# Batch 0 of a fused linear-attention and Swish kernel: by tiles, or by pairs of heads

## The chip, the cores and the metric

The kernel runs on one core of a Trainium2 chip. The metric is device microseconds of one execution. Before the change five runs gave a median of 295.37 us (295.13 to 296.06). Engines are called as in the profile: PE (TensorE), PEld (its weight loads), DVE (VectorE), ACT (ScalarE), POOL (GpSimd), SP (SyncE, which here only issues DMAs).

## The reference

Linear attention with phi(x) = elu(x) + 1, and behind it a feed-forward layer with a Swish whose slope differs per hidden unit:

```python
# q, k, v: (8 batches, 8 heads, 576, 64); w_in: (512, 2048); w_out: (2048, 512); beta: (2048,)
q_p, k_p = phi(q), phi(k)                       # phi(x) = where(x > 0, x, exp(x) - 1) + 1
kv  = einsum('bhsd,bhse->bhde', k_p, v)
z   = sum(k_p, axis=2)
num = einsum('bhsd,bhde->bhse', q_p, kv)
den = einsum('bhsd,bhd->bhs', q_p, z) + 1e-06
x   = (num / den) with the heads side by side   # (8 * 576, 512)
h   = x @ w_in
out = (h / (1 + exp(-beta * h))) @ w_out        # (4608, 512)
```

## The kernel before, in words

Everything is float32 in memory and bfloat16 on PE. A batch has 576 positions: four tiles of 128 and a tail tile of 64 (tile 4). The four tiles of a batch form xT[b], 512 channels by 512 positions; the tails of all eight batches are collected in xT_tail and computed as a ninth batch.

For each batch the order is: phi of k and q (an exp on ACT, a relu and a min on DVE: `phi_part`, `phi_relu`, `phi_min`, lines 134 to 154), kv and z on PE, numerators per tile on PE, the division by the denominator on DVE (`xs`), the transposes of x, then H: sixteen groups `ff` of 128 hidden units, each four matmuls over 512 positions (`h_mm`, line 321) and a Silu on ACT (`silu`), and then Y: four tiles, each four times four matmuls (`y_mm`, line 338), a copy out of PSUM and two output DMAs (`y_out`). Beta is folded in by scaling the Silu's input with beta and w_out's rows with 1/beta (`w_out_scale`).

The schedule is written out by hand: each engine runs its instructions in the order of the code, and waits on semaphores alone. From batch 2 on the attention steps of the next batch are put between the groups of H and Y by tables `sh` and `sy` (lines 629 to 652). Batches 0 and 1 are laid out by hand (lines 438 to 593), and the change is mostly there.

Loads. k of batch 0 goes by SP in float32 into `stage`, in two halves of four heads (line 93). q, v and all weights go by POOL's DMA queue, which casts to bfloat16: identities first (lines 98 to 101), then q and v of batch 0 in halves (lines 110 to 113), w_in in four quarters (line 118), later w_out, k, q and v of batches 1 and 2 (lines 447 to 452 and 531 to 533).

Heads. The 128 partitions hold two heads of 64 positions; index `hh` is the head's half on the partitions and `pr` a pair of heads on the free side, so `pr` = 0 gives channels 0 to 255 of x and `pr` = 1 channels 256 to 511 (`kc` = 0, 1 and 2, 3 of w_in).

Batch 0 in order on PE (lines 475 to 518): transposes of q for tiles 0 and 1 (`q_trans0`, copies on ACT), kv of pair 0 (`kv_direct` into kvp0), q's tile 2, den of tiles 0 and 1 (`dens`, then `recips` on DVE), kv of pair 1 (into kvp1), q's tile 3, numerators of tiles 0 and 1 (`numer0`: all 512 channels of a tile, one DVE multiplication into xs), q's tile 4, den of tiles 2 to 4, x's transposes of tiles 0 and 1 (`x_trans`, copies on ACT) around the numerators of tiles 2 and 3, then `h0_tile`: the first four groups of H tile by tile, 16 matmuls of 128 positions for each, with the transposes of tiles 2 and 3 (copies on DVE) and the numerator of tile 4 between. Then the four Silus, and groups 4 to 15 with all 512 positions; before group 6 stand the transposes of tile 4. PSUM has four buffers of tag "mm" in turn (warm_ps, two kvp0, dps, then the four h_ps, and so on), two "misc" ones for transposes and two "num0" ones for numerators: a later user of a buffer waits for the earlier one's reader.

Batch 0's Y and batch 1's attention are interwoven by hand (lines 537 to 593): Y's groups i = 0, 1 of all four tiles, group 2 of tile 0, z of batch 1, transposes of q for tiles 0 to 3, group 2 of tiles 1 and 2, q's tile 4, kv, den, `recips` and `kv_evac` on DVE, group 2 of tile 3 and group 3 of tile 0, the first numerators of batch 1.

ACT holds one table of functions at a time: in the profile an ACT_TABLE_LOAD stands where it changes between Exp and Silu. Copies run under either.

Of the kernel before, what the change touches and what calls it, by code (L numbers as in the profile page):

```python
# [16 lines left out]
def kernel(  # L17
# [61 lines left out]
    def load(eng, dst, src, b, h0=0, n=4):  # L79

        rows = src[b].rearrange("h (g j) d -> (h g) (j d)", j=J)
        return eng.dma_start(  # L82
            out=dst[:, h0 : h0 + n].rearrange("p h j d -> p h (j d)"),
            in_=rows.rearrange("(i p) e -> p i e", p=P)[:, h0 : h0 + n],
        )
# [9 lines left out]
    nc.vector.memset(warm, 0.5)  # L95
    tiny = consts.tile([P, 2], BF16)
    nc.scalar.activation(tiny[:, 0:1], warm[:, 0:1], ACTF.Exp)
    identity = consts.tile([P, P], BF16)
    make_identity(nc, identity)
    ident16 = consts.tile([FC, FC], F32)  # L100
# [7 lines left out]
    for i in range(2):  # L108
        nc.vector.memset(vaug[i][:, :, :, :, D : D + 2], 1.0)
    for h0 in (0, 2):  # L110
        load(nc.gpsimd, xq[0], q, 0, h0, 2)
    for h0 in (0, 2):
        load(nc.gpsimd, vb[0], v, 0, h0, 2)

    w_in_v = moe_w_in.rearrange("(c p) f -> p c f", p=P)
    w_out_v = moe_w_out.rearrange("(c p) m -> p c m", p=P)
    for i in range(4):
        nc.gpsimd.dma_start(out=w_in_sb[i], in_=w_in_v[:, :, i * 512 : (i + 1) * 512])

    def load_w_out(i):  # L120
        nc.gpsimd.dma_start(out=w_out_f[i], in_=w_out_v[:, i * 4 : (i + 1) * 4, :])
# [291 lines left out]
    def num0_tile():  # L413
        return num0ps.tile([P, 512], F32, tag="num0", name="nps0")
# [43 lines left out]
    idle(4)  # L458
    z_products(0, 1, zt)
    nc.vector.tensor_copy(beta_s, bps)  # L460
    nc.vector.tensor_mul(beta_m, beta_s, beta_s)
    nc.vector.tensor_scalar(beta_m, beta_m, TINY * TINY, 2.0 * TINY, ALU.is_lt, ALU.mult)
    nc.vector.tensor_add(beta_c, beta_s, beta_m)
    phi_step("q", 0, phi_relu)
    z_evac(zt)
    phi_step("q", 0, phi_min)
# [5 lines left out]
    def q_trans0(t):  # L472
        q_trans(0, (t,), misc_bf()[:, 0 : 512 if t < NT - 1 else 256], (nc.scalar,))

    q_trans0(0)
    q_trans0(1)
    kv_direct(0, 0, kvp0)
    for hh in range(2):
        kv_evac(0, hh, (0,), kvp0)
    q_trans0(2)  # L480
    dens(0, (0, 1), dps)
    recips(0, 2, P, dps)
    kvp1 = [num0_tile() for _ in range(2)]
    kv_direct(0, 1, kvp1)
    for hh in range(2):
        kv_evac(0, hh, (1,), kvp1)
    q_trans0(3)
    numer0(0, 0)
    numer0(0, 1)
    q_trans0(4)  # L490
    dens(0, (2, 3, 4), dps)
    x_trans(0, 0, nc.scalar)
    recips(2, 4, P, dps)
    recips(4, 5, G, dps)
    numer0(0, 2)
    x_trans(0, 1, nc.scalar)
    numer0(0, 3)
    hps = [mm_tile("h_ps") for _ in range(4)]

    def h0_tile(t):  # L500
        for ff in range(4):
            h_mm(0, xT[0], ff, hps[ff], t * P, (t + 1) * P)

    h0_tile(0)
    x_trans(0, 2, nc.vector)
    x_trans(0, 3, nc.vector)
    h0_tile(1)
    numer0(0, 4)
    h0_tile(2)
    h0_tile(3)  # L510
    for ff in range(4):
        silu(0, ff, hps[ff])
    for ff in range(4, FC):
        if ff == 6:
            x_trans(0, 4, nc.vector)
        hp = mm_tile("h_ps")
        h_mm(0, xT[0], ff, hp)
        silu(0, ff, hp)

    def w_out_scale(i, n_act):  # L520
        for c in range(4):
# [21 lines left out]
    kv1 = [miscps.tile([P, 512], F32, tag="misc", name="kv1") for _ in range(2)]  # L543
    kv_tile(1)
    y_mm(0, 0, 2, yps[0])
    for pr in range(2):
        z_products(1, pr, kv1)
    z_evac(kv1)
    w_out_scale(3, 0)
    for ts in ((0, 1), (2, 3)):  # L550
        q_trans(1, ts, num0_tile().bitcast(BF16), (nc.scalar, nc.scalar))
    y_mm(0, 1, 2, yps[1])
    y_mm(0, 2, 2, yps[2])
    dps1 = num0_tile()
    q_trans(1, (4,), dps1.bitcast(BF16)[:, 512:768], (nc.scalar,))
    for pr in range(2):
# [3 lines left out]
    recips(4, 5, G, dps1)  # L560
    for hh in range(2):
        kv_evac(1, hh, (0, 1), kv1)
    y_mm(0, 3, 2, yps[3])
    y_mm(0, 0, 3, yps[0])
    y_out(0, 0, yps[0], copier=nc.scalar)
    numer0(1, 0)
# [116 lines left out]
```

## Time and profile before

| what | value |
|---|---|
| median of 5 runs | 295.37 us (295.13 to 296.06) |
| the profiled execution | 296.06 us, its span 294.3 us |
| busy share of the span | PE 97%, PEld 49%, ACT 54%, DVE 40%, POOL 12% |
| matmuls of y (L341) | x600, 127.1 us busy, 370 ns of one |
| matmuls of h (L323) | x560 with xT, 118.3 us busy; x64 with the tails, 14.0 us |
| Silu (L331) | x144, 98.3 us busy, 688 ns of one |
| xs (L288, DVE) | x40, 27.2 us busy, 687 ns of one |
| first matmul of H in batch 0 | 17.11 us |
| first matmul of Y in batch 0 | 32.54 us |
| last piece of the chain that ended last | 290.14 us, copy of y on DVE |

All times in the timeline are microseconds from the span's start. A timeline row gives start, length from first start to last end, engine, line, operation, output and inputs, shape, how many instructions the row merges (x16), and in brackets how long the engine had been idle before it and who released it. A matmul's own length (0.38 for 512 columns, 0.22 for 128) is longer than its distance to the next (0.216 and 0.056), since matmuls are pipelined. A row of POOL or SPq with DMA_DIRECT2D is the issue of a DMA; it lands much later: q's two halves of batch 0 took a median of 7.7 us from issue to landing, w_in's quarters 13.8 us, w_out's up to 21 us. The digits in the page's second part are tenths of each of 40 slices of 7.4 us.

### The profile page before, as it was taken

To read this page: it belongs to the slowest core of one execution; us is meant where nothing else is said; L and a number is where in the kernel's file an instruction comes from. 1 tells how busy PE (TensorE), PEld (TensorE's weight loads), DVE (VectorE), ACT (ScalarE), POOL (GpSimd) and SP (SyncE) were. 2 spreads that over 40 slices of the span, in tenths; PEclk is the share of its full clock that TensorE was granted. 3 is DMA by queue.
4 is the path that set the end of the run, shared out by engine and by line. 5 is a ranking of instruction groups with operands and counts; after the bars stand their busy time and mean duration, and the time that the engine had idled before them with its cause. 6 is when DMAs were issued, how large, how long until landed. Compare 5 with 4: busy or idle time off the path is not lost.

```text
span 294.3 us, 4755 instructions
## 1 busy us (share of the span) xinstructions
PE 286.1 (97%) x1889; PEld 143.7 (49%) x1889; DVE 116.7 (40%) x268; ACT 158.6 (54%) x206; POOL 36.7 (12%) x54
## 2 busy tenths in 40 slices
PE   8899999999999999999999999999999999999994
PEld 3584457454445444544455445544554444444443
DVE  5663575835634461356135613652251200110021
ACT  5558685963936772578167916690671077017500
POOL 9532100320050005000500053000000000000000
PEclk9999999999999999999999999999999999999998
DMA  7999999489389949942993299717131310130033
GB/s 202 200 213 393 251 251 191 101 247 195 76 159 278 165 78 270 217 66 66 246 245 70 53 197 262 106 45 154 38 71 45 74 36 0 39 87 19 0 71 75
DMA packets 50887, 40.83 MB, mean 139 GB/s; under 512 B 30752, under 2 KB 42288, under 8 KB 50864
## 3 DMA queue, kind: packets, MB, share of 16 engines
q1 hardware_dynamic: 37968, 23.48, 33.8%
q0 software_dynamic: 12736, 16.91, 29.6%
q8 instruction: 15, 0.25, 0.3%
q10 hardware_dynamic: 160, 0.13, 0.2%
q14 instruction: 8, 0.07, 0.1%
HBM read 36.71 MB, written 9.44 MB: 157 GB/s over the span
## 4 chain that ended last, share of the span: by engine, by line
PE 84%; DMA 11%; ACT 2%; DVE 1%; POOL 1%; issue 1%; POOLq 0%; ACTq 0%
PE y_ps L341 39%; PE h_ps L323 38%; DMA xk<-in_k_dram 7%; DMA vf<-in_v_dram 3%; PE nps L274 2%; PE kvp L173 2%; ACT e L138 1%; POOL xq L82 1%; PE nps L421 0%; ACT L138 0%; PE xtp L304 0%; PE kv L184 0%; PE nps L242 0%; DVE y_sb L231 0%; DVE xs L288 0%
## 5 line engine op out<-in xcount | busy, mean ns | idle before, releaser
L331 ACT ACTIVATE g<-h_ps,beta_c 128x512 bf16<-128x512 f32 x144 | 98.3, 688 | 100.0 <-PE h_ps L323 100.0
L341 PE MATMUL y_ps<-w_out,g 128*128 128x512 bf16 (+3 forms) x600 | 127.1, 370 | 0.0
L323 PE MATMUL h_ps<-xT,w_in 128*128 128x512 bf16 (+1 forms) x560 | 118.3, 361 | 0.5 <-DVE y_sb L231 0.2
L341 PEld LDWEIGHTS <-g 128*128 128x128 bf16 x600 | 58.1, 98 | 64.7
L323 PEld LDWEIGHTS <-w_in 128*128 128x128 bf16 x624 | 56.7, 98 | 59.1 <-issue 0.7
L231 DVE COPY y_sb<-y_ps 128x512 f32<-128x512 f32 (+2 forms) x36 | 24.0, 672 | 82.5 <-PE y_ps L341 82.5
L288 DVE TENSOR_TENSOR xs<-nps,rden 128x512 bf16<-128x512 f32 (+1 forms) x40 | 27.2, 687 | 3.4 <-PE nps L421 1.8
L138 ACT ACTIVATE e<-xq 128x1152 bf16<-128x1152 bf16 (+2 forms) x17 | 18.0, 1100 | 2.3 <-DMA xq<-in_q_dram 2.3
L82 POOL DMA_DIRECT2D xk<-in_k_dram x7 | 5.2, 745 | 108.0 <-DMA qTd<-phi_q 81.3
L149 DVE TENSOR_TENSOR phi_q<-e,r 128x1152 bf16<-128x1152 bf16 (+2 forms) x17 | 12.1, 722 | 15.9 <-ACT e L138 15.6
L223 DVE TENSOR_TENSOR kv_bd<-kvp,kvmask 128x260 bf16<-128x260 f32 x12 | 4.6, 423 | 27.4 <-PE kvp L173 27.4
L138 ACT ACTIVATE e<-xk 128x1152 bf16<-128x1152 bf16 x14 | 15.4, 1149 | 0.0
L323 PE MATMUL h_ps<-xT_tail,w_in 128*128 128x512 bf16 x64 | 14.0, 379 | 0.0
L282 DVE TENSOR_SCALAR den<-nps 128x8 f32<-128x8 f32 (+1 forms) x30 | 4.9, 164 | 22.3 <-PE nps L274 22.3
L274 PEld LDWEIGHTS <-qTd 128*128 128x128 bf16 x120 | 9.3, 98 | 7.7 <-DVE xs L288 0.9
L149 DVE TENSOR_TENSOR phi_k<-e,r 128x1152 bf16<-128x1152 bf16 x16 | 11.5, 751 | 2.5 <-ACT e L138 2.3
L274 PE MATMUL nps<-kv_bd,qTd 128*128 128x130 bf16 x120 | 11.9, 221 | 0.4 <-DVE xs L288 0.4
L163 POOL CAST vaug<-vf 128x1152 bf16<-128x1152 f32 x10 | 11.2, 1159 | 2.2 <-DMA vf<-in_v_dram 2.2
L138 ACT ACT_TABLE_LOAD x6 | 7.7, 1283 | 5.6 <-DMA xq<-in_q_dram 3.8
L127 PE MATMUL warm_ps<-warm 128*128 128x512 bf16 x28 | 8.6, 465 | 1.5 <-DVE warm L95 1.5
L331 ACT ACT_TABLE_LOAD x7 | 9.0, 1283 | 0.1
L173 PEld LDWEIGHTS <-phi_k 64*128 64x128 bf16 x216 | 6.3, 94 | 2.5 <-issue 2.5
(69 smaller groups left out, 107.2 us busy)
## 6 DMA issues: line engine op xcount, KB each, us to landing
out_dram<-y_sb SPq DMA_DIRECT2D x70, 128.0 KB, 2.4
vf<-in_v_dram SPq DMA_DIRECT2D x5, 1152.0 KB, 6.2
xk<-in_k_dram POOLq DMA_DIRECT2D x7, 576.0 KB, 10.2
xq<-in_q_dram POOLq DMA_DIRECT2D x7, 576.0 KB, 13.0
w_in<-in_moe_w_in_dram POOLq DMA_DIRECT2D x4, 512.0 KB, 13.8
g<-in_moe_w_out_dram POOLq DMA_DIRECT2D x2, 1024.0 KB, 17.7
stage<-in_moe_w_out_dram POOLq DMA_DIRECT2D x2, 1024.0 KB, 21.0
stage<-in_k_dram SPq DMA_DIRECT2D x2, 576.0 KB, 4.1
```

Of the source, the lines that this page charges most:

```text
L82: return eng.dma_start(out=dst[:, h0 : h0 + n].rearrange("p h j d -> p h (j d)"), in_=rows.rearrange("(i p) e -> p i e", p=P)[:, h0 : h0 + n],
L127: nc.tensor.matmul(warm_ps[:, 0:cols], warm[:, 0:P], warm[:, 0:cols], start=True, stop=True)
L138: nc.scalar.activation(st[b, a, pr, "e"][:, :, j0:j1], x[:, :, j0:j1], ACTF.Exp)
L149: nc.vector.tensor_tensor(st[b, a][:, pr, j0:j1].rearrange("p j (h d) -> p j h d", h=2), st[b, a, pr, "e"][:, :, j0:j1].rearrange("p h j d ...
L163: eng.tensor_copy(vaug[b % 2][:, pr, :, :, 0:D], src[:, 2 * pr : 2 * pr + 2].rearrange("p h j d -> p j h d"),)
L173: nc.tensor.matmul(ps[hh, pr], st[b, "k"][r, pr, j, :], vaug[b % 2][r, pr, j, :, 0:EA], start=(j == 0), stop=(j == J - 1), skip_group_chec ...
L231: eng.tensor_copy(dst, src)
L274: nc.tensor.matmul(nps[: qs.shape[-1], hh, pr * 2 * EA : (pr + 1) * 2 * EA], qs, st[b, "kv"][:, hh, pr, :], start=True, stop=True, skip_gr ...
L288: nc.vector.tensor_mul(xs[:n].rearrange("p i a d -> p a i d"), num, rd[:, :, :, None].to_broadcast([n, 2, 4, D]),)
L323: nc.tensor.matmul(hp[:, c0:c1], w_in_sb[ff // 4][:, kc, (ff % 4) * P : (ff % 4 + 1) * P], x[:, kc, c0:c1], start=(kc == 0), stop=(kc == K ...
L331: nc.scalar.activation(g_sb[b % 2][:, ff, :], hp, ACTF.Silu, scale=beta_c[:, ff : ff + 1])
L341: nc.tensor.matmul(yp[:, c0:c1], g_sb[b % 2][:, ff, t * P : (t + 1) * P], w_out_sb[i][:, c, c0:c1], start=(ff == 0), stop=(ff == FC - 1), ...
```

## The change

Five edits:

- q's two loads of batch 0 are issued on POOL ahead of the identities and not behind them. w_in's first quarter is loaded in two calls, channels 0 to 255 and 256 to 511.
- Batch 0's tiles 0 to 3 go by halves of 256 channels. `numer_part` makes the numerators of two tiles for one pair of heads (and two half-width multiplications on DVE), `x_part` transposes one half of a tile (two transposes, one copy of 128x256, always on ACT), `h0_part` adds one half of a tile to the first four groups of H (eight matmuls). kv of pair 1 goes into the other columns of kvp0. den of tiles 0 and 1 now comes before q's tiles 2 and 3. A one-column Silu behind the second half copy loads ACT's table there. The three small DVE instructions for beta go behind the last multiplication.
- Tile 4 of batch 0 (q's transposes, den, numerator, x's transposes) moves into the groups of H behind `ff` = 5, 7, 8 and 10.
- In batch 0's Y, group 2 of tile 1 moves ahead of batch 1's z, group 2 of tile 2 ahead of the transposes of q, group 2 of tile 3 ahead of q's tile 4 (from behind `kv_evac`).
- In batch 1's H, kv of batch 2 goes behind group 8 and not 9, and the numerators start behind group 10 and not 11; the fourth and fifth and the DMA transposes of x follow in the groups of Y.

```diff
@@ loads @@
     nc.scalar.activation(tiny[:, 0:1], warm[:, 0:1], ACTF.Exp)
+    for h0 in (0, 2):
+        load(nc.gpsimd, xq[0], q, 0, h0, 2)
     identity = consts.tile([P, P], BF16)
     make_identity(nc, identity)
...
-    for h0 in (0, 2):
-        load(nc.gpsimd, xq[0], q, 0, h0, 2)
...
     for i in range(4):
-        nc.gpsimd.dma_start(out=w_in_sb[i], in_=w_in_v[:, :, i * 512 : (i + 1) * 512])
+        for c0, c1 in ((0, 2), (2, KC)) if i == 0 else ((0, KC),):
+            nc.gpsimd.dma_start(
+                out=w_in_sb[i][:, c0:c1], in_=w_in_v[:, c0:c1, i * 512 : (i + 1) * 512]
+            )
@@ batch 0 @@
     nc.vector.tensor_copy(beta_s, bps)
-    nc.vector.tensor_mul(beta_m, beta_s, beta_s)
-    nc.vector.tensor_scalar(beta_m, beta_m, TINY * TINY, 2.0 * TINY, ALU.is_lt, ALU.mult)
-    nc.vector.tensor_add(beta_c, beta_s, beta_m)
...
+    def numer_part(ts, pr):
+        nps = num0_tile()
+        for i, t in enumerate(ts):
+            for hh in range(2):
+                nc.tensor.matmul(
+                    nps[:, (i * 2 + hh) * P : (i * 2 + hh + 1) * P].rearrange(
+                        "p (h d) -> p h d", h=2
+                    ),
+                    q_stat(0, t, hh, pr, P),
+                    st[0, "kv"][:, hh, pr, :].rearrange("p (h e) -> p h e", h=2)[:, :, 0:D],
+                    start=True, stop=True, skip_group_check=True,
+                )
+        for i, t in enumerate(ts):
+            if pr == 0:
+                st[0, "xs", t] = work.tile([P, 4, 2, D], BF16, tag="xs", name="xs", bufs=4)
+            nc.vector.tensor_mul(
+                st[0, "xs", t][:, 2 * pr : 2 * pr + 2].rearrange("p i a d -> p a i d"),
+                nps[:, i * 256 : (i + 1) * 256].rearrange("p (a h d) -> p a h d", a=2, h=2),
+                rden0[:, t, :, 2 * pr : 2 * pr + 2, None].to_broadcast([P, 2, 2, D]),
+            )
+
+    def x_part(t, pr):
+        xv = st[0, "xs", t].rearrange("p i a d -> p (i a d)")
+        tp = misc_bf()[:, 0:256].rearrange("p (c t) -> p c t", c=2)
+        for c in range(2):
+            nc.tensor.matmul(
+                tp[:, c], xv[:, (2 * pr + c) * P : (2 * pr + c + 1) * P], identity,
+                is_transpose=True, start=True, stop=True, skip_group_check=True,
+            )
+        nc.scalar.copy(xT[0][:, 2 * pr : 2 * pr + 2, t * P : (t + 1) * P], tp)
+
+    def h0_part(t, pr):
+        for ff in range(4):
+            for kc in range(2 * pr, 2 * pr + 2):
+                nc.tensor.matmul(
+                    hps[ff][:, t * P : (t + 1) * P],
+                    w_in_sb[0][:, kc, ff * P : (ff + 1) * P],
+                    xT[0][:, kc, t * P : (t + 1) * P],
+                    start=(t == 0 and kc == 0), stop=(t == 3 and kc == KC - 1),
+                    skip_group_check=True,
+                )
...
     for hh in range(2):
         kv_evac(0, hh, (0,), kvp0)
-    q_trans0(2)
     dens(0, (0, 1), dps)
     recips(0, 2, P, dps)
-    kvp1 = [num0_tile() for _ in range(2)]
-    kv_direct(0, 1, kvp1)
+    q_trans0(2)
+    q_trans0(3)
+    numer_part((0, 1), 0)
+    kv_direct(0, 1, kvp0)
+    dens(0, (2, 3), dps)
     for hh in range(2):
-        kv_evac(0, hh, (1,), kvp1)
-    q_trans0(3)
-    numer0(0, 0)
...
+        kv_evac(0, hh, (1,), kvp0)
     recips(2, 4, P, dps)
...
+    x_part(0, 0)
+    x_part(1, 0)
+    nc.scalar.activation(tiny[:, 1:2], warm[:, 0:1], ACTF.Silu)
+    numer_part((0, 1), 1)
+    numer_part((2, 3), 0)
     hps = [mm_tile("h_ps") for _ in range(4)]
...
+    h0_part(0, 0)
+    x_part(0, 1)
+    h0_part(1, 0)
+    x_part(1, 1)
+    numer_part((2, 3), 1)
+    nc.vector.tensor_mul(beta_m, beta_s, beta_s)
+    nc.vector.tensor_scalar(beta_m, beta_m, TINY * TINY, 2.0 * TINY, ALU.is_lt, ALU.mult)
+    nc.vector.tensor_add(beta_c, beta_s, beta_m)
+    h0_part(0, 1)
+    x_part(2, 0)
+    h0_part(1, 1)
+    x_part(3, 0)
+    h0_part(2, 0)
+    x_part(2, 1)
+    h0_part(3, 0)
+    x_part(3, 1)
+    h0_part(2, 1)
+    h0_part(3, 1)
     for ff in range(4):
         silu(0, ff, hps[ff])
     for ff in range(4, FC):
-        if ff == 6:
-            x_trans(0, 4, nc.vector)
         hp = mm_tile("h_ps")
         h_mm(0, xT[0], ff, hp)
         silu(0, ff, hp)
+        if ff == 5:
+            q_trans0(4)
+        if ff == 7:
+            dps4 = num0_tile()
+            dens(0, (4,), dps4)
+            recips(4, 5, G, dps4)
+        if ff == 8:
+            numer0(0, 4)
+        if ff == 10:
+            x_trans(0, 4, nc.vector)
@@ batch 0's Y @@
     y_mm(0, 0, 2, yps[0])
+    y_mm(0, 1, 2, yps[1])
     for pr in range(2):
         z_products(1, pr, kv1)
     z_evac(kv1)
     w_out_scale(3, 0)
+    y_mm(0, 2, 2, yps[2])
     for ts in ((0, 1), (2, 3)):
         q_trans(1, ts, num0_tile().bitcast(BF16), (nc.scalar, nc.scalar))
-    y_mm(0, 1, 2, yps[1])
-    y_mm(0, 2, 2, yps[2])
+    y_mm(0, 3, 2, yps[3])
     dps1 = num0_tile()
...
         kv_evac(1, hh, (0, 1), kv1)
-    y_mm(0, 3, 2, yps[3])
     y_mm(0, 0, 3, yps[0])
@@ from batch 1 on @@
         if n < B:
-            at(sh, 9 if b == 1 else 4, lambda: kv_both(n))
+            at(sh, 8 if b == 1 else 4, lambda: kv_both(n))
             for t in range(NT):
-                ff = (11 if b == 1 else 5) + 2 * t
-                side, i = (sh, ff) if ff < FC else (sy, ff - FC - 1)
-                at(side, i, lambda t=t: numer(n, t))
-                side, i = (sh, ff + 1) if ff + 1 < FC else (sy, ff - FC + 1)
-                at(side, i, lambda t=t: x_trans_dma(n, t))
+                ff = (10 if b == 1 else 5) + 2 * t
+                for g, f in ((ff, numer), (ff + 1, x_trans_dma)):
+                    at(*((sh, g) if g < FC else (sy, g - FC)), lambda t=t, f=f: f(n, t))
```

More of the change, by code (lines that the diff above doesn't have):

```diff
@@ L479 @@
         kv_evac(0, hh, (0,), kvp0)
-    q_trans0(2)
     dens(0, (0, 1), dps)
     recips(0, 2, P, dps)
-    kvp1 = [num0_tile() for _ in range(2)]
-    kv_direct(0, 1, kvp1)
-    for hh in range(2):
-        kv_evac(0, hh, (1,), kvp1)
-    q_trans0(3)
-    numer0(0, 0)
[L489 to L492, printed above, removed]
-    recips(2, 4, P, dps)
[L494 to L497, printed above, removed]
-    hps = [mm_tile("h_ps") for _ in range(4)]
[L500 to L510, printed above, removed]
+    q_trans0(2)
[3 more added lines that the diff above has]
+    dens(0, (2, 3), dps)
+    for hh in range(2):
+        kv_evac(0, hh, (1,), kvp0)
+    recips(2, 4, P, dps)
+    x_part(0, 0)
[3 more added lines that the diff above has]
+    numer_part((2, 3), 0)
+    hps = [mm_tile("h_ps") for _ in range(4)]
+    h0_part(0, 0)
[16 more added lines that the diff above has]
+    h0_part(3, 1)
     for ff in range(4):
```

## The prediction

> **What bounds the kernel now.** I read the page first. TensorE is busy 97% of the span and nearly full in every slice, so only stretches where PE waits can give time back: the start, and a few holes behind it. The start is fed by a DMA system that is full from the second slice on.
>
> ```profile
> PE 286.1 (97%) x1889; PEld 143.7 (49%) x1889; DVE 116.7 (40%) x268; ACT 158.6 (54%) x206; POOL 36.7 (12%) x54
> PE   8899999999999999999999999999999999999994
> DMA  7999999489389949942993299717131310130033
> ```
>
> Then I read the timeline of the first 22 us. The reader is to see who releases whom: k's loads are issued at 0.74 and q's at 1.62, ScalarE (ACT) gets q only at 9.00, PE the first whole transposes of q at 11.91, and ACT then serves PE with copies until it loads Silu's table at 17.57, which costs nothing there since VectorE (DVE) does the last two copies of x.
>
> ```profile
> 0.74 0.96 SPq L82 DMA_DIRECT2D stage<-in_k_dram  x2
> 1.62 1.55 POOL L82 DMA_DIRECT2D xq<-in_q_dram  x2
> 9.00 1.16 ACT L138 ACTIVATE e<-xq 128x1152 bf16<-128x1152 bf16 x1 [1.99 <-DMA xq<-in_q_dram]
> 11.91 0.51 PE L242 MATMUL tp<-identity,phi_q 128*128 128x128 bf16 x6 [0.61 <-DVE phi_q L149]
> 12.23 1.75 ACT L229 COPY qT<-tp 128x512 bf16<-128x512 bf16 x3 [0.53 <-PE tp L242]
> 15.40 0.37 ACT L229 COPY qT<-tp 128x256 bf16<-128x256 bf16 x1 [0.22 <-PE tp L242]
> 17.57 1.28 ACT L331 ACT_TABLE_LOAD   x1
> 21.12 3.58 ACT L331 ACTIVATE g<-h_ps,beta_c 128x512 bf16<-128x512 f32 x6 [2.27 <-PE h_ps L323]
> ```
>
> Last, the timeline of 40 to 73 us, for the two holes that the other edits touch: batch 1's transposes wait for phi_q at 41.69, and the fourth numerator of batch 2 waits at 70.92 for xs. Between them lies a chain that is now just covered: den at 46.41 to kv_bd's end at 47.85, beside eight matmuls of y that end at 47.97.
>
> ```profile
> 41.69 0.96 PE L242 MATMUL nps<-identity,phi_q 128*128 128x128 bf16 x14 [0.41 <-DVE phi_q L149]
> 46.23 1.90 PE L341 MATMUL y_ps<-w_out,g 128*128 128x512 bf16 x8
> 46.41 0.19 DVE L410 TENSOR_SCALAR den<-nps 128x32 f32<-128x32 f32 x1 [3.05 <-PE nps L403]
> 47.15 0.70 DVE L208 TENSOR_TENSOR kv_bd<-kv,kvmask 128x256 bf16<-128x256 f32 x2
> 47.97 0.63 PE L421 MATMUL nps<-kv_bd,qT 128*128 128x128 bf16 x8
> 70.92 0.41 PE L274 MATMUL nps<-kv_bd,qTd 128*128 128x130 bf16 x4 [0.36 <-DVE xs L288]
> ```
>
> **The change part by part.** The sum is made against the profiled execution, 296.06 us with a span of 294.3. Pitches from the timeline: a 128x512 matmul 0.216 (four are 0.86), a 128x128 one 0.056, so eight of a half group take 0.44.
>
> *1. q ahead of the identities.* q's issue moves from 1.62 to 0.73, past two memsets and two selects (0.9 on POOL); these now end at about 3.2, and the first user of an identity is at 6.88. SP's queue keeps k at 0.74. What follows q in POOL's queue (v, w_in) is issued as before, so only q can gain. What an earlier issue is worth is not in the trace. At best 0.89, if all goes by issue time. At least 0: no byte of q moved before 5.0, when k's were done, and it may be so again. The windows show 385 GB/s from 2.75 to 5.0 (k, float32), 151 from 5.0 to 6.5, and about 200 afterwards, counted at q's bf16 size. So the slow start of q's stream costs some (207-151)/207 x 1.5 = 0.4. If q's first packets ride under k's tail, most of that goes: I take -0.3, nearest to that row. The chain q, exp, min, transposes moves by the same amount.
>
> The Trainium skill ("DMA: Bandwidth & Descriptors", section on queues, rings and completion order) says that each DMA engine goes round robin over the queues that have work. By that rule q would have shared from about 2.6 on; the trace has q's first packets at 5.0, and the row decides. By the rule this term would be near -0.9.
>
> *2. w_in in two calls.* One more issue of 0.75 on POOL (8.01 to 8.76); POOL's next issue waits until 9.26 now, and the DMA queue is 11 to 16 us of work ahead, which is what covers it. The first half lands about 14.6 instead of 15.85; nothing needs it before 16. Cost 0. beta's three DVE instructions (0.18 each) go behind xs, end near 19, and are hidden by the wait for the first Silu at 21.1. If not, that Silu is late by as much.
>
> *3. Batch 0 in halves.* I lay out the new order from the rows, q unmoved. PE transposes tiles 0 and 1 at 11.91, does kv at 12.35, and den of tile 1 waits for the second copy (13.31), so the transposes of tiles 2 and 3 start at 13.55 behind it instead of 12.96. Their copies end at 14.55 and 15.05. The first half numerator is at 14.0, kv's second half at 14.25 to 14.85, den of tile 3 at 15.1 behind the copy, the first two half transposes of x at 15.3. Their copies (0.37 each, the 128x256 row) end at 15.95 and 16.2. Then ACT loads Silu's table: 1.28, and a 0.21 Activate, until 17.7. Behind it in ACT's queue stand the other six copies of x; the first (tile 0's second half) ends at 18.0. PE has by then done two half groups, two half transposes and a numerator, the last at 17.3, and waits 0.7: the new wait, in front of everything else on PE. From 18.04 there remain 56 matmuls of 0.056, 3.1, and four or five round trips PE, ACT, PE of 0.04+0.37+0.05, each covered by 0.44 of matmuls except some 0.06: the last ends at 21.4. The first Silu starts six matmuls before it instead of twelve, so the fifth group, which needs its PSUM buffer, waits 0.6 instead of 0.27 and starts at 22.0, where it starts at 21.86 now. **+0.14**. The table load has no row at such a place. Its lower bound is the whole wait gone, -0.7; upward, copies as long as the 128x512 ones (0.59) would add 0.22 at four places, +0.9. I keep the 0.37 row, since the shape is the same.
>
> The Trainium skill ("ScalarE: Activation LUTs", section on what a table load costs) puts 1.28 for the load and 1.38 for a drain on each switch, which speaks against a load in mid stream. This trace agrees with the 1.28, but the load at 17.57 starts 0.02 after a copy's end, and the exp after the one at 35.23 starts 0.01 after its end. By the page the sum would be 1.4 more.
>
> *4. Tile 4 into the groups of h.* Two transposes (0.11), four thin den matmuls with their edges (0.3; 15.82 to 16.04 now) and the half-width numerator (19.29 to 19.79 now, 0.44 net). They leave the start, which item 3 counts, and cost PE **+0.85** between groups; ACT's copy of 0.37 fits, as a Silu takes 0.69 of each 0.86. Bounds 0.6 and 1.1. So y starts 1.0 later.
>
> *5. y's groups moved.* Two groups (1.73) now stand before batch 1's transposes, so these start near 43.7, and phi_q (41.63) is no longer awaited: the wait of 0.6 (first two transposes over at 41.1, the next at 41.69) goes, **-0.6**. It would have gone to item 4's delay anyway. But one group instead of two stands between den and batch 1's first numerator: den's end to kv_bd's end is 1.56, the cover 0.86. PE's next instruction, with everything queued behind it, waits **+0.7** (bounds 0.3, if the first half of kv_bd releases all, and 0.86).
>
> *6. Batch 2's numerators one group earlier.* Now eight matmuls stand between the third and the fourth, as between the others, which show no wait. PE ended its four at 70.39 and started at 70.92: **-0.5** (bounds 0 and -0.53). kv at group 8 starts near 61.6; phi_k is done at 59.97 and v's copy at 54.2, so this has cover of 1.6.
>
> Sum: 0.14 + 0.85 - 0.6 + 0.7 - 0.5 = +0.6 with q unmoved, and **+0.3** with q 0.3 earlier: 296.4 for an execution like the profiled one. That one is the slowest of the five shown, 0.7 above their median, so I put the sum on the median: 295.37 + 0.3 = **295.7**. 0.2%, or 0.59 us, is about what a measurement of this kernel can tell from no change.
>
> **The rivals.** *Faster.* q goes by issue time (-0.9) and the table load hides (-0.7 of item 3): 0.6 - 1.6 = -1.0, 294.4; with q alone -0.3, 295.1, which is no change. For it: the load now hides, and 0.5 of ACT idle time precedes the third half copy. Against: that idle time is a third of what the load takes.
>
> *Slower: ACT's copies become the bound of batch 0.* Place: the six half copies behind the table load. Price: up to 0.9 on top of +0.3, 296.6. It decides as soon as a copy with its two hand-overs passes the 0.44 of matmuls that cover it. For it: 0.46 against 0.44 is no margin at all, and eight copies all fall to ACT, where DVE did half. Against: the 0.37 row has that very shape.
>
> *It doesn't do what it says.* q lands at 8.98 and 10.42 as before because k's packets hold the engines. Then +0.6, 296.0, on the edge of what can be told.
>
> **How the numbers follow.** Forecast, with its neighbours inside 0.59: 0.40. q unmoved: 0.18, halved between same and slower. ACT the bound: 0.24. Faster: 0.18. So faster 0.18, same 0.49, slower 0.33. The forecast's own range is 295.1 to 296.0; the wider one reaches into both outer cases, 294.7 to 296.6.
>
> **What would show it.** q's exp before 8.8 (item 1). ACT's table load between copies at about 15.9, and PE idle for some 0.7 behind it, released by xT's copy; the fifth group of h near 21.7 (item 3). y's first matmul 0.5 to 1.0 later than 32.54 (items 3 and 4). No idle time before the transposes of batch 1, and a new one of about 0.7 before its first numerator, released by kv_bd (item 5). No idle time at the fourth numerator of batch 2 (item 6). The prediction is wrong if h's fifth group starts before 21.2 or after 22.3, or if den to kv_bd is covered.

## The result, and the profile after

The changed kernel takes a median of **295.87 us** (295.35 to 296.64, 30 runs), the kernel before in the same comparison 295.47 (295.12 to 296.07, 50 runs). The ratio is 1.0014 with a 95% interval of 1.0009 to 1.0019: 0.4 us slower, and less than the 0.59 us that the prediction takes for no change. The profiled execution took 296.52 us with a span of 294.8 us, where before's took 296.06 with 294.3.

The page's busy shares and slices, as shown for the kernel before:

```profile
PE 287.0 (97%) x1889; PEld 143.8 (49%) x1889; DVE 116.4 (39%) x270; ACT 160.1 (54%) x213; POOL 37.2 (13%) x55
PE   8989999999999999999999999999999999999994
DMA  8999999389569939962993299618131310130032
```

Almost nothing moves here: the second slice of PE gains a tenth and the third loses one. A change that shifts waits of half a microsecond has to be read from the timeline. Its first 24 us, with the rows that answer to those of before:

```profile
1.24 1.53 POOL L82 DMA_DIRECT2D xq<-in_q_dram  x2 [0.80 <-POOLq L720]
7.60 1.16 ACT L141 ACTIVATE e<-xq 128x1152 bf16<-128x1152 bf16 x1 [0.83 <-DMA xq<-in_q_dram]
11.21 0.61 PE L245 MATMUL tp<-identity,phi_q 128*128 128x128 bf16 x8
14.85 0.65 ACT L505 COPY xT<-tp 128x256 bf16<-128x256 bf16 x2 [0.48 <-PE tp L501]
15.52 1.28 ACT L536 ACT_TABLE_LOAD   x1
16.92 0.63 ACT L505 COPY xT<-tp 128x256 bf16<-128x256 bf16 x2
17.33 0.61 PE L511 MATMUL h_ps<-xT,w_in 128*128 128x128 bf16 x8 [0.45 <-ACT xT L505]
20.55 3.58 ACT L334 ACTIVATE g<-h_ps,beta_c 128x512 bf16<-128x512 f32 x6 [0.36 <-PE h_ps L511]
21.29 1.89 PE L326 MATMUL h_ps<-xT,w_in 128*128 128x512 bf16 x8 [0.44 <-ACT g L334]
```

q's exp starts at 7.60 instead of 9.00, but the transposes of q gain less: the third of them, the first that needs the second piece of phi_q, starts at 11.32 (two pitches into the row at 11.21) instead of 11.91. ACT loads its table between two pairs of half copies, and PE waits behind it at 17.33, in front of everything that PE has still to do. The fifth group of H starts at 21.29 (21.86 before).

The timeline from 43 to 88 us, with the two places that the prediction named and one that it did not:

```profile
43.00 1.06 PE L245 MATMUL nps<-identity,phi_q 128*128 128x128 bf16 x16
...
46.78 1.04 PE L344 MATMUL y_ps<-w_out,g 128*128 128x512 bf16 x4
46.96 0.19 DVE L413 TENSOR_SCALAR den<-nps 128x32 f32<-128x32 f32 x1 [2.92 <-PE nps L406]
47.71 0.69 DVE L211 TENSOR_TENSOR kv_bd<-kv,kvmask 128x256 bf16<-128x256 f32 x2
48.13 0.83 PE L424 MATMUL nps<-kv_bd,qT 128*128 128x128 bf16 x8 [0.31 <-DVE kv_bd L211]
...
70.76 0.40 PE L277 MATMUL nps<-kv_bd,qTd 128*128 128x130 bf16 x4
75.82 0.83 DVE L145 TENSOR_SCALAR r<-xq 128x1152 bf16<-128x1152 bf16 x2 [3.50 <-DMA xq<-in_q_dram]
...
87.30 1.89 PE L326 MATMUL h_ps<-xT,w_in 128*128 128x512 bf16 x8 [0.37 <-DVE y_sb L234]
```

The sixteen transposes of batch 1 at 43.00 wait for nothing any more. The one group of y at 46.78 does not cover the chain from den to kv_bd, and the first numerator waits. The fourth numerator of batch 2 at 70.76 has lost its wait. But at 87.30 stands a new one, in front of the fourth group of batch 2's H, for a copy of y out of PSUM.

How far the changed kernel is ahead or behind, step by step: q's transposes -0.59; the fifth group of H -0.57; y's first matmul +0.32 (32.86 against 32.54); batch 1's H +0.37 (53.45 against 53.08); batch 2's first Silu -0.17 (85.24 against 85.41); its fifth +0.36 (89.22 against 88.86); the end of the span +0.45.

### The profile page after: what moved, and what is told of

It is laid out like the page before. It is cut to its first block, busy times and chain, and to the rows that moved or that the text cites. A ratio compares the mean times of both kernels' runs of the same rounds, so it can differ in the third digit from the quotient of the medians.

```text
span 294.8 us, 4767 instructions
## 1 busy us (share of the span) xinstructions
PE 287.0 (97%) x1889; PEld 143.8 (49%) x1889; DVE 116.4 (39%) x270; ACT 160.1 (54%) x213; POOL 37.2 (13%) x55
## 4 chain that ended last, share of the span: by engine, by line
PE 86%; DMA 6%; ACT 2%; DVE 2%; issue 2%; SPq 0%; POOL 0%; DVEq 0%; POOLq 0%; ACTq 0%
PE h_ps L326 37%; PE y_ps L344 37%; DMA xq<-in_q_dram 4%; PE warm_ps L130 3%; PE kvp L176 2%; PE nps L277 2%; DMA qTd<-phi_q 1%; PE h_ps L511 1%; DMA out_dram<-y_sb 1%; DVE y_sb L234 1%; ACT e L141 1%; PE nps L424 1%; PE kv L187 1%; PE xtp L307 0%; ACT L536 0%
## 5 line engine op out<-in xcount | busy, mean ns | idle before, releaser
L326 PE MATMUL h_ps<-xT,w_in 128*128 128x512 bf16 x496 | 115.0, 379 | 1.2 <-DVE y_sb L234 0.6
L326 PEld LDWEIGHTS <-w_in 128*128 128x128 bf16 x560 | 52.7, 98 | 59.0 <-issue 1.7
L291 DVE TENSOR_TENSOR xs<-nps,rden 128x512 bf16<-128x512 f32 (+1 forms) x36 | 24.7, 689 | 4.3 <-DMA xT<-xs 1.8
L130 PE MATMUL warm_ps<-warm 128*128 128x512 bf16 x28 | 9.3, 496 | 1.5 <-DVE warm L95 1.5
L145 DVE TENSOR_SCALAR r<-xq 128x1152 bf16<-128x1152 bf16 x16 | 7.0, 466 | 3.5 <-DMA xq<-in_q_dram 3.5
```

The costliest lines, as they stand in the source:

```text
L130: nc.tensor.matmul(warm_ps[:, 0:cols], warm[:, 0:P], warm[:, 0:cols], start=True, stop=True)
L145: nc.vector.tensor_scalar(r, x, 0.0, 1.0, ALU.max, ALU.add)
L291: nc.vector.tensor_mul(xs[:n].rearrange("p i a d -> p a i d"), num, rd[:, :, :, None].to_broadcast([n, 2, 4, D]),)
L326: nc.tensor.matmul(hp[:, c0:c1], w_in_sb[ff // 4][:, kc, (ff % 4) * P : (ff % 4 + 1) * P], x[:, kc, c0:c1], start=(kc == 0), stop=(kc == K ...
```

## The experiments

The theory: the time is a sum of small terms, each at its own place on PE's path. q earlier gives a few tenths; the halves together with tile 4 in H cost about 0.9 before y; the move of y's groups takes one wait away that the delay would have covered anyway, and adds one of 0.7; earlier numerators give up to 0.5. The rivals: that a term is hidden and moves nothing when it is undone, and that what one step gains is given back by a later wait. "Before" below is before's median in the same runs.

### One part alone: q ahead of the identities, and the earlier numerators

The first kernel is before with q's two loads ahead of the identities:

```diff
     nc.scalar.activation(tiny[:, 0:1], warm[:, 0:1], ACTF.Exp)
+    for h0 in (0, 2):
+        load(nc.gpsimd, xq[0], q, 0, h0, 2)
     identity = consts.tile([P, P], BF16)
...
     for h0 in (0, 2):
-        load(nc.gpsimd, xq[0], q, 0, h0, 2)
-    for h0 in (0, 2):
         load(nc.gpsimd, vb[0], v, 0, h0, 2)
```

> The kernel before, with only q's two loads of batch 0 moved ahead of the identities. Theory: the earlier issue is worth far more than the 0.3 us that I forecast. q's halves land 1.4 us earlier as in the changed kernel (7.6 and 9.0 for 8.98 and 10.42), PE starts the whole transposes of q about 0.7 earlier (11.2 for 11.91), the rest of POOL's loads follow 0.65 earlier and with them phi_q of batch 1, so nothing takes the gain back: 294.8 us, ratio 0.998. Rival 1: q is held behind k all the same and the earlier landing came from the other edits: 295.5, ratio 1.000. Rival 2: the start is 0.7 earlier but PE waits as much longer for phi_q of batch 1 at about 41.7: ratio 1.000 with a gap of 1.2 there.

Measured: 295.09 against 295.49, ratio 0.9988 (0.9979 to 0.9996), by which it gains 0.36 us. Its timeline:

```profile
8.01 1.16 ACT L138 ACTIVATE e<-xq 128x1152 bf16<-128x1152 bf16 x1 [0.99 <-DMA xq<-in_q_dram]
9.23 2.10 PE L127 MATMUL warm_ps<-warm 128*128 128x512 bf16 x9 [0.16 <-issue]
11.17 0.61 PE L242 MATMUL tp<-identity,phi_q 128*128 128x128 bf16 x8
```

Of the 0.99 that q's exp gains on the profiled execution of before, 0.63 arrive at the third transpose (11.28): PE's idle matmuls, the last of which starts at 10.96, stand in the way until 11.17. Between two profiled executions this is not a fixed figure. q lands at 8.98, 8.06 and 8.74 in three profiled kernels that load it behind the identities (mean 8.6), and between 7.39 and 8.07 in ten that load it ahead (mean 7.7). The gain at the landing is thus nearer to 0.9 than to the 1.41 of the two executions that the result compares. At the third transpose the means of the same profiles are 11.65 and 11.10 (without the last kernel below, which has fewer idle matmuls), so 0.55 arrive there, and what it is worth in the time is the 0.36 of the ratio. Where the last 0.2 goes was not traced; it is within the interval.

The second kernel is before with the edit in batch 1's H alone:

```diff
-            at(sh, 9 if b == 1 else 4, lambda: kv_both(n))
+            at(sh, 8 if b == 1 else 4, lambda: kv_both(n))
             for t in range(NT):
-                ff = (11 if b == 1 else 5) + 2 * t
+                ff = (10 if b == 1 else 5) + 2 * t
```

(and the lines for H and Y as in the change.)

> The kernel before, with only batch 1's H changed: kv of batch 2 behind group 8, numerators from group 10. Theory: the wait of 0.5 at the fourth numerator goes, but the DMA transposes of x start 0.5 earlier and run into the load of q of batch 3, which lands some 2 us later (75.8 for 73.9); DVE waits for it in order, its copies of y come 2 us later, and PE waits 0.5 to 0.6 in batch 2's H near 87: in all 0, ratio 1.000. Rival: the late load and the wait at 87 come from the other edits (the whole front being 0.4 later), and this edit alone gains its 0.5: ratio 0.998.

Measured: 295.17, ratio 0.9991 (0.9981 to 1.0001), by which it gains 0.27 us, where the forecast had 0.5; the interval, 0.56 to nothing, holds both. In its trace, too, PE waits at batch 2's fourth group (0.3), so there part of the gain is given back.

### One part undone: y's groups back, Silu's table earlier

The changed kernel with the groups of y where they were:

```diff
     y_mm(0, 0, 2, yps[0])
-    y_mm(0, 1, 2, yps[1])
...
     w_out_scale(3, 0)
-    y_mm(0, 2, 2, yps[2])
     for ts in ((0, 1), (2, 3)):
         q_trans(1, ts, num0_tile().bitcast(BF16), (nc.scalar, nc.scalar))
-    y_mm(0, 3, 2, yps[3])
+    y_mm(0, 1, 2, yps[1])
+    y_mm(0, 2, 2, yps[2])
...
         kv_evac(1, hh, (0, 1), kv1)
+    y_mm(0, 3, 2, yps[3])
```

> The changed kernel, with the groups of batch 0's Y where they were before. Theory: phi_q of batch 1 is ready at 41.0 in the changed kernel, before PE can be there (41.3), so moving the groups bought nothing and costs the wait of 0.68 for kv_bd at 48: 0.7 us less than the changed kernel, 295.2, ratio 0.999 to the kernel before. Rival: the wait for phi_q comes back (0.6) and the time is that of the changed kernel, 295.9, ratio 1.0014.

Measured: 295.15, ratio 0.9988 (0.9978 to 0.9997), where the change has 1.0014: 0.72 us between the medians. The timeline of this kernel:

```profile
40.70 1.27 PE L245 MATMUL nps<-identity,phi_q 128*128 128x128 bf16 x16
45.73 0.19 DVE L413 TENSOR_SCALAR den<-nps 128x32 f32<-128x32 f32 x1 [3.05 <-PE nps L406]
47.29 0.63 PE L424 MATMUL nps<-kv_bd,qT 128*128 128x128 bf16 x8
```

With two groups of y behind den the numerator at 47.29 waits for nothing, as before the change. The transposes at 40.70 now show no wait either, although the groups are back behind them: y starts at 32.30, too little ahead of phi_q (ready at 40.96) to wait for more than 0.2 of it. So the wait for phi_q, which the move was to remove, had gone by itself, and the move only bought the wait for kv_bd.

The changed kernel with the Silu that loads the table moved up behind q's last exp:

```diff
     phi_step("q", 1, phi_part, 4, J)
+    nc.scalar.activation(tiny[:, 1:2], warm[:, 0:1], ACTF.Silu)
...
     x_part(1, 0)
-    nc.scalar.activation(tiny[:, 1:2], warm[:, 0:1], ACTF.Silu)
```

> The changed kernel, with the one-column Silu that loads ACT's table moved up behind the last exp of q, into 1.4 us in which ACT is idle. Theory: the wait of 0.62 on PE behind the table load goes, nothing takes its place but round trips of 0.06: 0.5 to 0.6 less than the changed kernel, 295.3, ratio 0.9995. Rival: the half copies themselves bound batch 0 (0.46 a round trip against 0.44 of matmuls), and the wait moves to the last pieces: at most 0.2 less, 295.7, ratio 1.001.

Measured: 295.68, ratio 1.0012 (1.0003 to 1.0022): 0.2 below the change's median, within the two intervals. Its timeline:

```profile
10.18 1.28 ACT L449 ACT_TABLE_LOAD   x1
11.58 1.05 ACT L232 COPY qT<-tp 128x512 bf16<-128x512 bf16 x2
16.64 0.61 PE L512 MATMUL h_ps<-xT,w_in 128*128 128x128 bf16 x8
```

The wait for the half copies is gone: from the second half group to the third it is 0.79 (15.85 to 16.64) instead of 1.40. But the first copies of q now stand behind the load: from the third transpose (11.00) to the first half group it is 4.27 instead of 4.03. Of 0.6, 0.24 is given back, and the fifth group still waits 0.44 for the first Silu. In the stretch from the third transpose to y's first matmul this is worth 0.36 (21.54 to 21.18), and 0.13 in a later kernel with the same edit.

### The new wait at 87 us

In the trace of the change the four DMA transposes of x of batch 2 take longer, and q of batch 3 lands later: 75.80 instead of 73.89. The DMA view of 66 to 76 us has one row for these transposes; its number is the median from issue to landing. First before, then after:

```profile
xT<-xs SPq DMA_TRANSPOSE x4, 4.9
```

```profile
xT<-xs SPq DMA_TRANSPOSE x4, 7.0
```

The first of them is issued 0.5 earlier (66.47, before 66.97), while the load of q of batch 3 is issued 0.4 later (64.91, before 64.53), so more of the two streams runs side by side. DVE's queue holds q's relu (75.82, idle 3.50 ahead of it; before 73.92) in front of the copies of y, the last of which ends 1.9 later, and with it the PSUM buffer of a group of H comes free late. For this last copy the way from q leads through SP's queue, which has the transposes of phi_q in front of the output DMAs of y:

```profile
80.23 2.81 SPq L260 DMA_TRANSPOSE qTd<-phi_q  x2
86.55 0.69 DVE L234 COPY y_sb<-y_ps 128x512 f32<-128x512 f32 x1 [1.50 <-DMA out_dram<-y_sb]
```

The copy waits for an output DMA to free one of the three buffers of y_sb. These transposes start at 78.33 in before, and there the last copy, at 84.62, waits only for y itself. The pattern holds over the runs. In the six kernels with the earlier numerators and batch 3's k first, q of batch 3 takes 10.7 to 11.4 from issue to landing and PE waits 0.3 to 1.0 at this group; in the three with the numerators as before, q takes 9.4 to 9.6 and that wait is absent. The changed kernel with batch 3's q loaded ahead of its k, as a test:

```diff
-            d = load(nc.gpsimd, xk[b % NX], k, b)
+            first = b == 3
+            d = load(nc.gpsimd, xq[b % NX] if first else xk[b % NX], q if first else k, b)
...
-            load(nc.gpsimd, xq[b % NX], q, b)
+            load(nc.gpsimd, xk[b % NX] if first else xq[b % NX], k if first else q, b)
```

> The changed kernel, with batch 3's q loaded ahead of its k (these two loads alone change places). Theory: the wait of 0.4 to 1.0 near 87 comes from DVE standing at q of batch 3 (landing at 75.8 with k first) with the copies of y queued behind; with q landing near 71 DVE is never held, and the wait goes: 0.5 us less than the changed kernel, 295.3, ratio 0.9995 to the kernel before. Rival: what holds the last copy of y at 86.5 is the output DMAs on SP, which release its buffer late behind the transposes; then the wait stays and the time is 295.9, ratio 1.0014.

Measured: 295.70, ratio 1.0013 (1.0004 to 1.0022), against 1.0014 for the change: no gain. Its timeline shows the mechanism all the same:

```profile
71.99 0.82 DVE L145 TENSOR_SCALAR r<-xq 128x1152 bf16<-128x1152 bf16 x2
83.93 4.48 PE L326 MATMUL h_ps<-xT,w_in 128*128 128x512 bf16 x20
```

The relu is 3.8 earlier and twenty matmuls of H run without a wait. So the chain from q's landing to PE's wait is shown, but not that it costs the ordinary execution anything. The profiled executions hint at why, no more: three with a wait of 0.5 to 1.0 (the change, the kernel above with y's groups back, and one by tiles below) are 0.65, 0.75 and 0.44 above their own medians, while the three with a wait of 0.3 and the four with batch 3's q first are within 0.11 of theirs. But the profiled execution of before, without this wait, is 0.59 above its median (295.47) too. How often the two streams meet in executions without the profiler stays open.

### Halves or tiles

Before with nothing but tile 4 moved into the groups of H:

```diff
-    q_trans0(4)
-    dens(0, (2, 3, 4), dps)
+    dens(0, (2, 3), dps)
     x_trans(0, 0, nc.scalar)
     recips(2, 4, P, dps)
-    recips(4, 5, G, dps)
...
     h0_tile(1)
-    numer0(0, 4)
     h0_tile(2)
```

(and the steps of tile 4 behind groups 5, 7, 8 and 10, as in the change.)

> The kernel before, with only tile 4 of batch 0 moved into the groups of H (behind 5, 7, 8 and 10). From the rows: the start sheds 1.2 us (0.1, 0.66 with its wait, and 0.44) and H grows by 0.85, so from the transposes of q to y's first matmul it takes 0.3 less than the 20.6 to 20.7 of the kernels by tiles. Theory: PE then waits longer for phi_q of batch 1, which goes by the DMA queue, and 0 is left: 295.5, ratio 1.000. Rival: phi_q is no limit in most executions and 0.3 stays: 295.2, ratio 0.999.

Measured: 295.56, ratio 1.0003 (0.9994 to 1.0012). From the third transpose of q to the fifth group of H it takes 9.43 where before takes 9.95, and from there to y's first matmul 11.57 where before takes 10.68. So H pays 0.89 and the start gets back only 0.52. The timeline shows what tile 4 had been doing there:

```profile
15.56 0.40 PE L304 MATMUL xtp<-identity,xs 128*128 128x128 bf16 x4 [0.32 <-DVE xs L288]
```

With tile 4's transposes and den gone from the place ahead of it, PE waits for xs here: they had filled a hole. y is 0.38 later by this. That the median hardly moves fits batch 1's wait for phi_q swallowing it (in this trace PE doesn't wait there), but this isn't shown: in the six traces by tiles with tile 4 in the start the wait is anything from nothing to 0.6, 0.37 in the mean.

The whole stretch from the third transpose of q to y's first matmul separates the two forms of batch 0, since q's landing is outside it. It is 20.62 to 20.63 in before, in the two kernels of the first section, and in the three kernels by tiles below; 21.01 with tile 4 alone; 21.54 in the change, with y's groups back and with batch 3's q first; 21.18 and 21.41 in the two kernels with the table loaded early. The halves and tile 4 together cost 0.91, of which tile 4 has 0.38 and the halves 0.53.

A last attempt to save the halves: y's groups back, and tile 4 back in the start, its numerator in the wait behind the table load.

```diff
     numer_part((0, 1), 0)
+    q_trans0(4)
     kv_direct(0, 1, kvp0)
-    dens(0, (2, 3), dps)
+    dens(0, (2, 3, 4), dps)
...
     recips(2, 4, P, dps)
+    recips(4, 5, G, dps)
...
     numer_part((2, 3), 1)
+    numer0(0, 4)
```

(x's transposes of tile 4 stand before group 6 again.)

> The changed kernel with Y's groups back, and tile 4 of batch 0 back in the start: its transposes of q behind the first half numerators, its den with those of tiles 2 and 3, its numerator into the wait behind the table load, its transposes of x before group 6. Theory: tile 4 costs 0.85 in H and next to nothing where PE waits anyway; 0.4 to 0.6 less than the same kernel with tile 4 in H (0.9988): 294.6, ratio 0.997. Rival: ACT's extra copy (0.37) and DVE's extra multiplication (0.7) push the half copies back by as much: 295.1, ratio 0.999.

Measured: 295.29, ratio 0.9991 (0.9981 to 1.0001), not better than with y's groups back alone (0.9988). The stretch is 21.37 instead of 21.54:

```profile
16.01 1.28 ACT L538 ACT_TABLE_LOAD   x1
17.20 0.42 PE L424 MATMUL nps<-kv_bd,qT 128*64 128x128 bf16 x4
17.82 0.61 PE L511 MATMUL h_ps<-xT,w_in 128*128 128x128 bf16 x8 [0.20 <-ACT xT L505]
```

The numerator does stand in the hole, which shrinks from 0.45 to 0.20. But the table load starts 4.91 behind the third transpose of q and not 4.19 as with y's groups back alone, since the other steps of tile 4 now stand ahead of the first halves of x. The wait is filled with work that postpones what the wait is for.

### The better versions

The change with y's groups back, Silu's table early and batch 3's q first; beside it before (by tiles) with q first, the numerators earlier and batch 3's q first. Both put together edits shown above.

> The changed kernel with three repairs: Y's groups back where they were, Silu's table loaded behind the last exp of q, batch 3's q ahead of its k. If the repairs add up (0.75 as measured, 0.2 to 0.36, 0.5): 294.4, ratio 0.9965. If halves stay the more expensive form (21.2 from the transposes of q to y where tiles take 20.7), it is slower than the kernel before with the same repairs by 0.2 to 0.5; if it is the better form once ACT is no hindrance, it is the faster of the two.

> The kernel before by tiles, with q's loads ahead of the identities, batch 2's numerators one group earlier, and batch 3's q ahead of its k. Theory: 0.4 and 0.5 add up, since nothing holds DVE any more: 294.6, ratio 0.997, and no wait above 0.3 behind 30 us. Rival: the gain of the numerators is taken back near 87 all the same: 294.9, ratio 0.998.

Measured: by halves 294.98, ratio 0.9987 (0.9979 to 0.9996); by tiles 294.45, ratio 0.9969 (0.9958 to 0.9980). With the same repairs the tiles are 0.5 faster. The stretch has 0.78 between these two (21.41 and 20.63), the halves with the table early and tile 4 in H taken together. The last question was what is left to take by tiles. One kernel leaves out "batch 3's q first" from the version by tiles:

```diff
-            first = b == 3
-            d = load(nc.gpsimd, xq[b % NX] if first else xk[b % NX], q if first else k, b)
+            d = load(nc.gpsimd, xk[b % NX], k, b)
```

> The kernel before by tiles, with q's loads ahead of the identities and batch 2's numerators one group earlier, and batch 3's k still loaded ahead of its q. It differs from the run with 0.9969 by the order of those two loads alone. If the wait near 87 that DVE causes is worth something in a usual execution, this one is 0.3 to 0.5 slower than that: 294.8 to 294.9, ratio 0.998. If the order is worth nothing, as the changed kernel's medians say (1.0014 and 1.0013), it is 294.5, ratio 0.997.

Measured: 294.80 against a before of 295.69, ratio 0.9971 (0.9960 to 0.9983): the order of the two loads is worth nothing that shows. The other takes beta's steps and three idle matmuls out of the way of q's chain:

```diff
     z_products(0, 0, zt)
-    bps = miscps.tile([P, FC], F32, tag="misc", name="bps")
-    nc.tensor.matmul(bps, beta_row, ident16, is_transpose=True, start=True, stop=True)
     idle(4)
     z_products(0, 1, zt)
-    nc.vector.tensor_copy(beta_s, bps)
...
+    bps = miscps.tile([P, FC], F32, tag="misc", name="bps")
+    nc.tensor.matmul(bps, beta_row, ident16, is_transpose=True, start=True, stop=True)
     phi_step("q", 0, phi_relu)
+    nc.vector.tensor_copy(beta_s, bps)
...
-    idle(10)
+    idle(7)
```

(beta's other three steps on DVE go behind q's last min.)

> The version by tiles with 0.9969, and beyond it: beta's transpose behind z's second half and its small DVE steps behind phi_q, and seven matmuls in place of ten to keep PE awake ahead of q's transposes. Theory: phi_q's chain on DVE and PE's idle matmuls hold q's transposes some 0.3 to 0.4 back in the executions in which beta lands late (7.5) or PE's clock stays low longer: 294.1, ratio 0.9955. Rival: the shorter stretch of idle matmuls leaves PE at a low clock for the transposes and kv, and it gets slower: 295, ratio 0.9985.

Measured: 294.42, ratio 0.9960 (0.9947 to 0.9972). It is the fastest of all, 1.2 us below before by the ratio, though not told apart from the version by tiles without it (0.9969). In its trace the third transpose of q comes 2.93 after q's landing, 3.29 there; but PE then waits 0.51 for phi_q of batch 1, and nothing there.

## Why the prediction was right

**The sum.** +0.3 was forecast and +0.4 measured, inside the forecast's own range. The waits stand where they were forecast and have the releasers that were named; a further one, behind item 6, was not forecast. One sign missed: y's first matmul is 0.32 later in the profiled execution, where 0.5 to 1.0 was named, since q's transposes were 0.59 earlier there and not 0.3; counted from the third transpose it is 0.91 later.

A chain of kernels, each with one step more than the one ahead of it, leads from before to the change. By their ratios to before the steps are worth: q ahead of the identities -0.36 (0.9988), the earlier numerators -0.50 (0.9971), then the halves with tile 4 in H and w_in in two calls +0.50 (0.9988, the kernel with y's groups back), then y's groups +0.77 (1.0014). The forecast for these steps is -0.3, -0.5, +0.39 (the 0.99 of items 3 and 4 less the 0.6 for phi_q) and +0.7. Each step is uncertain by 0.3 to 0.4, so that the sum comes within 0.1 is partly luck.

**Item 1, q earlier.** Forecast -0.3, measured -0.36. The way there was partly different. The issue did not move to 0.73: POOL's first DMA stood until 1.24 behind memsets that end at 0.44, so q was issued 0.38 earlier and not 0.89. And the first packets of q still moved only when k was nearly done. What went is the slow start of q's stream, which the prediction had priced at 0.4. That term fits, but the step behind it, that the transposes move by the same amount, doesn't: of 0.9 at the landing 0.55 arrive at the third transpose, since PE's idle matmuls stand in the way in the first kernel above. The DMA view of 5.25 to 5.60 us gives the packets of POOL's queue. First before, then after:

```profile
q0 software_dynamic: 18, 0.02, 74.6%
```

```profile
q0 software_dynamic: 52, 0.06, 110.0%
```

The columns behind the name are packets, MB and share of the engines: 18 packets became 52, and 49 with q's edit alone; in all ten profiles with q ahead it is 47 to 52, in the three with q behind 9 to 22. From 4.4 to 4.9 us the queue moved no packet before and 2 after. The round robin over queues that the prediction takes from the Trainium skill ("DMA: Bandwidth & Descriptors", section on queues, rings and completion order) would have given q turns soon after its issue; again no run here shows that.

**Item 2, w_in in two calls.** Costed at nothing. No wait for w_in appears: the first half group runs behind its copies at 15.35. It was not tried alone. In the kernel with q alone ahead the undivided quarter lands at 14.85, ahead of 15.35 too.

**Item 3, the halves.** The order was laid out from rows of before, and it came out so: the table load between copies (forecast at 16.2 with q unmoved, 15.52 with q 0.6 earlier), PE's wait behind it (forecast 0.7; the matmul ahead of it starts at 16.66, 0.67 earlier, where a pitch is 0.06, so 0.61), the fifth group's wait for the first Silu (forecast 0.6; counted the same way, from the last matmul's start at 20.63, it is 0.60, while the 0.44 in the row counts from the modelled end of that matmul). The fifth group was forecast 0.14 later, q unmoved; against q's third transpose it is 0.02 later (9.97 against 9.95), so the term was 0.12 too high, and the shorter wait behind the table is 0.09 of it. ACT's copies did not become the bound: half groups follow each other at 0.55 to 0.62, where a half group and a pair of transposes take 0.55. The drain that the Trainium skill adds to each table switch ("ScalarE: Activation LUTs", section on what a table load costs) is not to be seen: the load runs from 15.52 to 16.80, and the next Activate starts at 16.81.

**Item 4, tile 4 in H.** Forecast +0.85, measured 0.89 in H in all six kernels that have it. Items 3 and 4 together: forecast +0.99, measured +0.91. What the prediction did not see is how this sum divides: it let the start lose all of tile 4's work, while 0.3 of it had filled a wait.

**Item 5, y's groups.** Forecast -0.6 and +0.7. The wait for kv_bd is 0.48 ahead of the first half of the numerator and 0.20 ahead of the second: 0.68. Taking it back gives 0.72. From y's start to batch 1's first numerator it is 15.43 before and 15.27 after, 15.47 if the second part of the wait is counted: +0.04, where +0.1 was forecast. The remark that the wait for phi_q "would have gone to item 4's delay anyway" is what the kernel with y's groups back shows (0.2 of that wait is left in its trace, 0.3 in the later version by halves), so the move itself is nearly all loss.

**Item 6, earlier numerators.** The wait went as forecast, and at batch 2's first Silu the trace gains the 0.54. What the prediction left out is that the DMA transposes are issued a group earlier too: in the traces they delay a load of q, and PE gives back 0.3 to 1.0 at batch 2's fourth group. The prediction had named no cover for them. Whether that makes the term smaller outside the profiler stays open. Alone it is worth 0.27, with q first 0.50, and the two are not told apart; and loading batch 3's q first, which removes the wait in the traces, changes neither ratio (1.0014 and 1.0013, 0.9971 and 0.9969).

**Items 3, 4 and 5 together.** Halves and tile 4 cost 0.91 before y in the traces and 0.50 in the ratios (0.9971 to 0.9988, two kernels that differ in nothing but batch 0's form, w_in's two calls and the place of beta's steps included). The wait for phi_q can take the difference, as the prediction has it, since it is 0 to 0.6 by tiles; how long it is in executions without the profiler was not measured.

**The rivals.** "Faster" needed q to gain 0.9 in the time, where it gained 0.36, and the table load hidden, which it was not: early, it delays the copies of q. "ACT's copies as the bound" did not occur. "q not earlier" did not occur, though the packets did wait for k's as it says.

## What to carry to other kernels

When several waits stand one behind the other on the bounding engine, price each edit as if the others were already in: a wait that an upstream delay swallows cannot be saved a second time, and moving cover work to save it opens a hole where the cover came from. Before taking work out of a stage that waits, look whether it fills the wait; before moving a step, follow its DMAs as far as its instructions. And compare a changed order in a stretch that starts behind the variable part (here q's landing), since there the same stretch repeated within 0.02 us in six kernels, while one pair of profiled executions overstated q's gain by half.

## What the runs showed of the hardware that was not expected

- POOL's first DMA issue starts at 1.24 or 1.25 in all ten profiles with q ahead of the identities, though POOL's last memset before it ends at 0.44. Behind the identities it starts at 1.62 in all three.
- While k's 1.18 MB in float32 move through SP's queue, POOL's queue gets next to nothing: q, issued at 1.24, had moved 2 packets by 4.9 us in the change and none in the other nine profiles with q ahead. Its issue time matters all the same for how fast it starts then (47 to 52 packets against 9 to 22 between 5.25 and 5.60). Why was not settled.
- The first idle matmuls of PE come at a pitch of 0.43 and later ones at 0.216, while the granted clock reads 1.00 there in all thirteen profiles. How many of the first fourteen are slow varies from 7 to 13 between profiles of nearly the same start, so the fourteenth starts anywhere from 5.87 to 6.98 us, and z behind it is shifted.
- The same four DMA transposes take a median of 4.9 us to landing before and 7.0 after, when they start 0.5 earlier beside a load that starts 0.4 later; that load lands 1.9 us later. Over the nine kernels with batch 3's k first, q takes 9.4 to 9.6 us to landing in three and 10.7 to 11.4 in the six that start the transposes earlier.
